# The last layer's bias for half the batch moves from matmuls into the factor

## The chip, the cores and the metric

The kernel runs on one core of one Trainium2 chip. The metric is the device time of one execution in microseconds (us), lower is better. A profile is one execution recorded by the hardware profiler; its span runs from the first to the last recorded instruction.

## The reference

A cross network of six layers over 4096 rows of 416 features, all in bf16:

```python
B, F, D, L = 4096, 26, 16, 6
Din = min(F * D, 1024)             # 416
x0: (B, Din)   ws: (L, Din, Din)   bs: (L, Din)

def reference(x0, ws, bs):
    x = x0
    for l in range(ws.shape[0]):
        x = x0 * (x @ ws[l] + bs[l]) + x
    return x
```

Every x is a product of x0 with a factor c: x = x0 * c, with c = 1 at the start and, after each layer, c = c + (x @ ws[l] + bs[l]). The kernel keeps c and forms x0 * c for the next layer's matmuls; the result is x0 times the last c.

## The kernel before

**Layout.** In layers 0 to 4 (L = 6, the last is `LL` = 5) features lie on partitions and batch rows in columns. The 416 features are three blocks of 128 (`m` or `k` = 0, 1, 2) and a remainder of 32. The batch is cut into two halves `s` = 0 and 1 of 2048 columns (`SW`), each of four groups `g` of 512 columns (`CW`). `CM[:, m, :]` holds the factor c for the blocks, `XM0` holds x0, and the `XH` buffers hold the products x0 * c that TensorE reads. The remainder lies in `CR` and `XR` with the four groups of a half on four groups of 32 partitions. `bM` and `bR` hold the biases of all layers in fp32, one value for each partition (one column for each layer), so the pair (`bM[:, m, l:l+1]`, or `bR[:, l:l+1]`) is a scalar for each partition.

**A layer from 1 to 4** has six tiles (s, m), in this order: (0,0), (0,1), (0,2), (1,0), (1,1), (1,2). The prediction calls them A, B, C, D, E, F, and the last of these layers (index 4, the fifth) layer five. They run in pairs: TensorE does the block matmuls of the first tile (`mm_full`, line 208), then the remainder's rows of the first and of the second (`mm_row`, line 214), then the block matmuls of the second. A tile's sums lie in two PSUM tiles (half `h` = 0 and 1, 1024 columns each). `ew_main` then does, for each half of a tile: ScalarE evicts PSUM into a buffer `t` and adds the bias (line 187); VectorE adds `t` to `CM` (line 188, the sum); VectorE multiplies `CM` by `XM0` into the next `XH` (line 189, the product). After the first pair, `rem_pair` does the remainder of both halves in the same way (`ew_rem`, lines 196, 202 and 203).

**What layer five adds.** The last layer is computed with batch rows on partitions, since the output has them so. So c is needed in rows too: after the eviction, sum and product of a tile's two halves, `xl_dmat` (line 231) issues one transposing DMA on SP's queue from `CM[:, m]` (2048 columns) into `XLrows`. For the remainder a transposing DMA goes from `CR` into `scrR[s]` (line 306), and ScalarE copies it into `XLrows` (`xl_rem`, line 313): for half 0 ahead of E's evictions, for half 1 after F's.

**The last layer.** Eight quads `q` = (s, i), four of each half; quad `q` covers four blocks of 128 batch rows (one in each group g), each with its own PSUM bank. They run two at a time (`rounds`: q = 0, 2, 4, 6), eight banks for each round. For each block TensorE multiplies the products (stationary) by the weights of the last layer (lines 361 and 367); `mm_q_rem` adds the remainder's features (line 379: four matmuls in four row groups) and the bias (line 382: four matmuls of a row of ones by the bias row `bLr`). ScalarE evicts into `t` (line 407), VectorE adds `XLrows` (line 409) and multiplies by x0 in rows into `o` (line 397), and a DMA on SP's queue writes `o` out. For the last three blocks of the last quad TensorE adds c itself (lines 371 and 373, by the identity), and the very last block is multiplied by VectorE straight from PSUM.

**What sets the order.** Each engine runs its instructions in one order. It follows the program's text; `pin` keeps the marked instructions in that order. SP's queue takes DMAs in the order in which they are issued. PSUM tiles come from one pool of four (two banks each), and `t` from a pool of six: a new tile waits until the one four, or six, before it has been read. The first eight banks of the last layer are those of E and F in layer five.

Of the kernel before, what the change touches and what calls it, by code (L numbers as in the profile page):

```python
# [9 lines left out]
ACT = mybir.ActivationFunctionType  # L10
ALU = mybir.AluOpType
BF16 = mybir.dt.bfloat16
FP32 = mybir.dt.float32
# [3 lines left out]
def kernel(  # L17
# [7 lines left out]
    nc = tc.nc  # L25
    B, D = x0.shape
    L = ws.shape[0]
    P = 128
    NK = 3
    R = D - NK * P  # L30
    assert R == 32 and B == 4096 and D == 416 and L >= 2
    NS = 2
    NG = 4
    CW = 512
    SW = NG * CW
    NBT = B // P
    LL = L - 1
# [3 lines left out]
    tpool = ctx.enter_context(tc.tile_pool(name="tpool", bufs=6))  # L41
    opool = ctx.enter_context(tc.tile_pool(name="opool", bufs=10))
    psum = ctx.enter_context(tc.tile_pool(name="psum", bufs=4, space=bass.MemoryType.PSUM))
# [8 lines left out]
    WR = const.tile([P, L, D], BF16)  # L52
# [3 lines left out]
    bM = const.tile([P, NK, L], FP32)  # L56
    bR = const.tile([P, L], FP32)
    X0rows = big.tile([P, NBT, D], BF16)
    XLrows = big.tile([P, NBT, D], BF16)
    scrR = [big.tile([P, 4, P], BF16, name=f"scrR{s}") for s in range(NS)]  # L60
# [3 lines left out]
    XM0 = big.tile([P, NK, B], BF16, name="XM0")  # L64
    XH = [big.tile([P, NK, SW], BF16, name=f"XH{i}") for i in range(3)]
    XR = [big.tile([P, NS * CW], BF16, name=f"XR{i}") for i in range(3)]
    CM = big.tile([P, NK, B], BF16, name="CM")
    CR = big.tile([P, NS * CW], BF16, name="CR")

    def col0(s, g):  # L70
        return SW * s + CW * g
# [8 lines left out]
    def pin(ins):  # L80
        tc.keep_in_program_order(ins)
# [94 lines left out]
    def ew_main(l, s, m, h, pt, nxt):  # L176
        c0 = col0(s, 2 * h)
        c, x = CM[:, m, c0:c0 + 2 * CW], nxt[s][:, m, 2 * CW * h:2 * CW * h + 2 * CW]
        src, bias = pt[:].rearrange("p a b -> p (a b)"), bM[:, m, l:l + 1]
        if l == 0:  # L180
            nc.scalar.activation(c, src, ACT.Identity, bias=bias, scale=1.0)  # L181
            for a in range(0, 2 * CW, CW):
                pin(nc.vector.tensor_tensor(out=x[:, a:a + CW], in0=c[:, a:a + CW],  # L183
                                            in1=XM0[:, m, c0 + a:c0 + a + CW], op=ALU.mult))
            return
        t = tpool.tile([P, 2 * CW], BF16, name="t")
        nc.scalar.activation(t[:], src, ACT.Identity, bias=bias, scale=1.0)  # L187
        nc.vector.tensor_tensor(out=c, in0=t[:], in1=c, op=ALU.add)  # L188
        nc.vector.tensor_tensor(out=x, in0=c, in1=XM0[:, m, c0:c0 + 2 * CW], op=ALU.mult)  # L189

    def ew_rem(l, s, pr, nxtR):
        cols = slice(CW * s, CW * s + CW)
        halves = [slice(a, a + CW // 2) for a in range(0, CW, CW // 2)]
        base = CR[:, cols] if l == 0 else tpool.tile([P, 2 * CW], BF16, name="t")
        for a in halves:
            nc.scalar.activation(base[:, a], pr[:, a], ACT.Identity, bias=bR[:, l:l + 1], scale=1.0)  # L196
        if l == 0:
            for a in halves:
                part = slice(CW * s + a.start, CW * s + a.stop)
                pin(nc.vector.tensor_tensor(out=nxtR[:, part], in0=CR[:, part], in1=XR[0][:, part], op=ALU.mult))  # L200
            return
        nc.vector.tensor_tensor(out=CR[:, cols], in0=base[:, 0:CW], in1=CR[:, cols], op=ALU.add)
        nc.vector.tensor_tensor(out=nxtR[:, cols], in0=CR[:, cols], in1=XR[0][:, cols], op=ALU.mult)

    def mm_full(l, s, m, g, pts, cur, first, last):
        for k in range(NK):
            for q in range(4):
                nc.tensor.matmul(pts[g // 2][32 * q:32 * q + 32, g % 2, :], lhsT=WM[:, l, k, 128 * m + 32 * q:128 * m + 32 * q + 32],  # L208
                                 rhs=cur[s][:, k, CW * g:CW * g + CW], start=(first and k == 0), stop=(last and k == NK - 1),
                                 tile_position=(0, 32 * q))  # L210

    def mm_row(l, s, m, pts, curR, first, last):
        for g in range(NG):
            nc.tensor.matmul(pts[g // 2][:, g % 2, :], lhsT=WR[32 * g:32 * g + 32, l, 128 * m:128 * m + 128],  # L214
                             rhs=curR[32 * g:32 * g + 32, CW * s:CW * s + CW],
                             start=first, stop=last, tile_position=(32 * g, 0))

    def mm_rem(l, s, pr, cur, curR):
        for g in range(NG):
            nc.tensor.matmul(pr[32 * g:32 * g + 32, :], lhsT=WD[:, l, g, :], rhs=curR[:, CW * s:CW * s + CW],  # L220
                             start=True, stop=False, tile_position=(0, 32 * g))
        for k in range(NK):
            for g in range(NG):
                nc.tensor.matmul(pr[32 * g:32 * g + 32, :], lhsT=WM[:, l, k, NK * P:D], rhs=cur[s][:, k, CW * g:CW * g + CW],  # L224
                      start=False, stop=(k == NK - 1), tile_position=(0, 32 * g))

    def new_pts():
        return [psum.tile([P, 2, CW], FP32, tag="ps", name=f"pt{h}") for h in range(2)]

    def xl_dmat(s, k):  # L230
        nc.sync.dma_start_transpose(out=XLrows[:, 16 * s:16 * s + 16, 128 * k:128 * k + 128],
                                    in_=CM[:, k, SW * s:SW * s + SW])
# [63 lines left out]
    for s in range(NS):  # L296
        first_layer(s)

    def rem_pair(l, cur, curR, nxtR, feeds_last):
        pr2 = psum.tile([P, 2, CW], FP32, tag="ps", name="pr2")  # L300
        for s in range(NS):
            mm_rem(l, s, pr2[:, s, :], cur, curR)
        for s in range(NS):
            ew_rem(l, s, pr2[:, s, :], nxtR)
            if feeds_last:
                nc.sync.dma_start_transpose(out=scrR[s][:], in_=CR[:, CW * s:CW * s + CW])

    def xl_rem(s):
        dst = XLrows[:, 16 * s:16 * s + 16, NK * P:D].rearrange("p (g i) r -> p i g r", g=NG)
        src = scrR[s][:].rearrange("p i (g r) -> p i g r", g=NG)  # L310
        n = 4 if s else 2
        for i in range(0, 4, n):
            pin(nc.scalar.copy(dst[:, i:i + n], src[:, i:i + n]))

    cur, curR = XH[0:2], XR[1]
    for l in range(1, LL):
        nxt, nxtR = [[h for h in XH if h is not cur[0] and h is not cur[1]][0], cur[0]], XR[1 + (l % 2)]
        feeds_last = (l == LL - 1)
        tiles = [(s, m) for s in range(NS) for m in range(NK)]
        pts = {}  # L320

        def finish(t):
            s, m = t
            for h in range(2):
                ew_main(l, s, m, h, pts[t][h], nxt)
            if feeds_last:
                xl_dmat(s, m)

        for n in range(0, len(tiles), 2):
            ta, tb = tiles[n], tiles[n + 1]  # L330
            pts[ta] = new_pts()
            for g in range(NG):
                mm_full(l, ta[0], ta[1], g, pts[ta], cur, True, False)
            mm_row(l, ta[0], ta[1], pts[ta], curR, False, True)
            pts[tb] = new_pts()
            mm_row(l, tb[0], tb[1], pts[tb], curR, True, False)
            if feeds_last and n == 4:
                xl_rem(0)
            finish(ta)
            for g in range(NG):  # L340
                mm_full(l, tb[0], tb[1], g, pts[tb], cur, False, True)
            finish(tb)
            if n == 0:
                rem_pair(l, cur, curR, nxtR, feeds_last)
        if feeds_last:
            xl_rem(1)
        cur, curR = nxt, nxtR

    l = LL
# [26 lines left out]
    def mm_q_rem(q, py, done):  # L376
        s, i = quads[q]
        for g in range(NG):
            nc.tensor.matmul(py[g][:, 0:D], lhsT=curR[32 * g:32 * g + 32, CW * s + 128 * i:CW * s + 128 * i + 128],  # L379
                             rhs=WR[32 * g:32 * g + 32, l, :], start=(g >= done), stop=False, tile_position=(32 * g, 0))  # L380
        for g in range(NG):
            nc.tensor.matmul(py[g][:, 0:D], lhsT=ones[32 * g:32 * g + 1, :],  # L382
                             rhs=bLr[32 * g:32 * g + 1, :], start=False, stop=(g < done), tile_position=(32 * g, 0))

# [32 lines left out]
    for q, at, done in rounds:  # L417
        tiles = [psum.tile([P, 2, CW], FP32, tag="ps", name=f"py{n}") for n in range(4)]
# [54 lines left out]
```

## Time and profile before

| | us |
|---|---|
| median of 3 runs | 130.15 (130.06 to 130.28) |
| profiled execution, device time | 129.88 |
| its span | 128.1 |
| TensorE busy | 123.6 |
| VectorE busy | 100.8 |
| ScalarE busy | 87.7 |

The granted TensorE clock is 1.0 throughout. The groups that the change touches, with count, busy time and mean duration of one, from the view of groups by form:

| line | engine, what | count | mean ns |
|---|---|---|---|
| 187 | ScalarE, eviction with bias, 128x1024 | 48 | 1114 |
| 188 | VectorE, sum, 128x1024 | 48 | 687 |
| 189 | VectorE, product, 128x1024 | 48 | 692 |
| 202, 203 | VectorE, remainder's sum and product, 128x512 | 8, 8 | 418, 425 |
| 379 | TensorE, remainder's features, last layer, 32x416 | 32 | 339 |
| 382 | TensorE, ones by bias, last layer, 1x416 | 32 | 335 |
| 407 | ScalarE, eviction, 128x832 and 128x416 | 9 and 13 | 855 and 505 |

A mean duration is not what an instruction costs its engine: the four matmuls of a group of line 379 or 382 run side by side, and one engine's instructions overlap at their ends, so the cost is read from the distance of starts.

### The profile page before, as it was taken

The numbers are of one execution on the slowest core, as the hardware profiler recorded it, in microseconds if no ns is written. First come the engines' busy times: TensorE is split into PE (matmuls) and PEld (weight loads), VectorE is DVE, ScalarE is ACT, GpSimd is POOL, SyncE is SP. The second block draws the span as 40 slices with busy tenths as digits, with TensorE's granted clock in tenths as the row PEclk, the third lists the DMA queues.
The fourth block names the chain that finished last, engine by engine and source line by source line (L and its number), as shares of the span: only waits on it lengthen the run. The fifth ranks groups of instructions, "written<-read, shape, count | busy, mean of one in ns | idle before, by whom it ended". The sixth has DMA issues, their size and how long they took to land.

```text
span 128.1 us, 4013 instructions
## 1 busy us (share of the span) xinstructions
PE 123.6 (97%) x1708; PEld 55.8 (44%) x1710; DVE 100.8 (79%) x195; ACT 87.7 (68%) x109; POOL 5.4 (4%) x18
## 2 busy tenths in 40 slices
PE   7999999999999999999999999999999999999980
PEld 3243443444544344434344434444434445445450
DVE  0034589774989898989898989898989899988991
ACT  0138857888858668858668858668858896569660
POOL 4004003400000000000000000000000000000000
PEclk9999999999999999999999999999999999999999
DMA  3999999999930000000000000000497899985764
GB/s 103 244 225 227 172 269 248 327 332 334 337 104 0 5 0 0 8 0 5 0 5 0 5 0 5 0 0 5 87 158 169 164 142 226 206 256 179 228 193 144
DMA packets 42230, 16.38 MB, mean 128 GB/s; under 512 B 31034, under 2 KB 42212, under 8 KB 42212
## 3 DMA queue, kind: packets, MB, share of 16 engines
q1 hardware_dynamic: 37432, 15.40, 53.2%
q10 hardware_dynamic: 4780, 0.72, 3.6%
q8 instruction: 13, 0.21, 0.7%
q14 instruction: 5, 0.04, 0.1%
HBM read 6.15 MB, written 3.41 MB: 75 GB/s over the span
## 4 chain that ended last, share of the span: by engine, by line
PE 96%; DVEq 1%; ACT 0%; issue 0%; DVE 0%
PE pt L208 50%; PE ph L240 12%; PE py L367 12%; PE pt L214 5%; PE pr L224 5%; PE wps L148 4%; PE pr L220 2%; PE py L379 1%; PE ph L247 1%; PE py L382 1%; PE py L361 1%; DVEq L468 1%; ACT t L407 0%; PE py L371 0%; PE tpr L163 0%
## 5 line engine op out<-in xcount | busy, mean ns | idle before, releaser
L208 PE MATMUL pt<-XH,WM 128*32 128x512 bf16 x1152 | 65.2, 379 | 0.0
L187 ACT ACTIVATE t<-pt,bM 128x1024 bf16<-128x1024 f32 x48 | 49.5, 1114 | 17.4 <-PE pt L214 17.4
L208 PEld LDWEIGHTS <-WM 128*32 128x32 bf16 x1152 | 29.7, 97 | 33.8 <-issue 5.1
L188 DVE TENSOR_TENSOR CM<-t,CM 128x1024 bf16<-128x1024 bf16 x48 | 33.0, 687 | 5.1 <-ACT t L187 5.1
L189 DVE TENSOR_TENSOR XH<-CM,XM 128x1024 bf16<-128x1024 bf16 x48 | 33.2, 692 | 3.6
L407 ACT CAST t<-py 128x416 bf16<-128x416 f32 (+1 forms) x22 | 14.3, 648 | 5.1 <-PE py L367 2.5
L367 PE MATMUL py<-WM,XH 128*128 128x416 bf16 x90 | 17.0, 339 | 0.0
L240 PE MATMUL ph<-XM,WM 128*128 128x512 bf16 x70 | 16.3, 380 | 0.1
L181 ACT ACTIVATE CM<-ph,bM 128x1024 bf16<-128x1024 f32 x12 | 12.5, 1113 | 3.5 <-PE ph L247 3.5
L183 DVE TENSOR_TENSOR XH<-CM,XM 128x512 bf16<-128x512 bf16 x24 | 8.8, 429 | 4.3 <-ACT CM L181 4.3
L367 PEld LDWEIGHTS <-XH 128*128 128x128 bf16 x90 | 8.5, 98 | 7.6 <-issue 1.4
L240 PEld LDWEIGHTS <-WM 128*128 128x128 bf16 x72 | 6.7, 98 | 8.4 <-issue 1.1
L409 DVE TENSOR_TENSOR t<-t,XLrows 128x416 bf16<-128x416 bf16 (+1 forms) x20 | 9.3, 468 | 1.1 <-ACT t L407 1.1
L397 DVE TENSOR_TENSOR o<-t,X0rows 128x416 bf16<-128x416 bf16 (+1 forms) x22 | 9.9, 457 | 0.1
L196 ACT ACTIVATE t<-pr,bR 128x256 bf16<-128x256 f32 x16 | 6.3, 474 | 2.1 <-PE pr L224 2.1
L214 PE MATMUL pt<-XR,WR 32*128 32x512 bf16 x96 | 7.3, 379 | 0.0
L224 PE MATMUL pr<-XH,WM 128*32 128x512 bf16 x96 | 6.6, 379 | 0.0
L114 ACT ACT_TABLE_LOAD x1 | 1.3, 1283 | 5.9 <-DMA XM<-in_x_dram 5.9
L224 PEld LDWEIGHTS <-WM 128*32 128x32 bf16 x120 | 3.2, 97 | 3.2
L157 DVE CAST bM<-pb 128x18 f32<-128x18 bf16 x1 | 0.2, 177 | 5.6 <-PE pb L156 5.6
L148 PE MATMUL wps<-const-float32-1.0 128*128 128x512 f32 x4 | 3.8, 1094 | 0.8 <-PEq L457 0.8
L220 PE MATMUL pr<-XR,WD 128*32 128x512 bf16 x40 | 3.9, 380 | 0.0
(53 smaller groups left out, 49.1 us busy)
## 6 DMA issues: line engine op xcount, KB each, us to landing
X0rows<-in_x_dram SPq DMA_DIRECT2D x8, 312.0 KB, 6.9
out_dram<-o SPq DMA_DIRECT2D x9, 208.0 KB, 3.3
WM<-in_ws_dram SPq DMA_DIRECT2D x5, 312.0 KB
out_dram<-o SPq DMA_DIRECT2D x13, 104.0 KB, 1.7
X0rows<-in_x_dram SPq DMA_DIRECT2D x4, 208.0 KB, 6.3
WR<-in_ws_dram SPq DMA_DIRECT2D x4, 130.0 KB, 5.3
WM<-in_ws_dram ACTq DMA_DIRECT2D x1, 312.0 KB
XM<-in_x_dram SPq DMA_TRANSPOSE x8, 5.5
```

The lines of the kernel that those rows point to most:

```text
L181: nc.scalar.activation(c, src, ACT.Identity, bias=bias, scale=1.0)
L187: nc.scalar.activation(t[:], src, ACT.Identity, bias=bias, scale=1.0)
L188: nc.vector.tensor_tensor(out=c, in0=t[:], in1=c, op=ALU.add)
L189: nc.vector.tensor_tensor(out=x, in0=c, in1=XM0[:, m, c0:c0 + 2 * CW], op=ALU.mult)
L208: nc.tensor.matmul(pts[g // 2][32 * q:32 * q + 32, g % 2, :], lhsT=WM[:, l, k, 128 * m + 32 * q:128 * m + 32 * q + 32], rhs=cur[s][:, k, C ...
L214: nc.tensor.matmul(pts[g // 2][:, g % 2, :], lhsT=WR[32 * g:32 * g + 32, l, 128 * m:128 * m + 128], rhs=curR[32 * g:32 * g + 32, CW * s:CW ...
L224: nc.tensor.matmul(pr[32 * g:32 * g + 32, :], lhsT=WM[:, l, k, NK * P:D], rhs=cur[s][:, k, CW * g:CW * g + CW], start=False, stop=(k == NK ...
L240: nc.tensor.matmul(pt[:, gl, :], lhsT=WM[:, 0, k, 128 * m:128 * m + 128], rhs=cur[:, k, c0:c0 + CW], start=(k == 0 and not after_row), sto ...
L367: nc.tensor.matmul(py[:, 0:D], lhsT=q_x(q, g, k), rhs=WM[:, l, k, :], start=((not closes) and k == 0), stop=(closes and not adds and k == ...
L397: pin(nc.vector.tensor_tensor(out=o[:, 0:n, :], in0=src, in1=X0rows[:, b, :], op=ALU.mult))
L407: nc.scalar.copy(tv, src)
L409: pin(nc.vector.tensor_tensor(out=tv, in0=tv, in1=XLrows[:, rows(q, g0, n), :], op=ALU.add))
```

## The change

In half 0 the last layer's bias is no longer added by TensorE. VectorE adds it to c in `CM` and `CR` in layer five, after the products that read c have been formed and before the transposing DMA takes c to rows: three tensor-with-scalar additions in place over 128x2048 (tiles A, B, C) and one over 128x512 (the remainder of half 0). In `mm_q_rem` the four matmuls by `ones` are left out for half 0 (the first four quads), and the remainder's matmuls close the accumulation there. Half 1 is as before.

Layer five gets a function of its own, `feeding_layer`, with VectorE's order written out and pinned. Sums stand ahead of products, other tiles' instructions stand between them, and the transposing DMAs of half 1 are issued after a tile's two sums, ahead of products. TensorE's order (`layer_products`) and ScalarE's order are those of before. On SP's queue the order is now A, remainder of half 0, B, remainder of half 1, C, D, E, F; before it was A, B, the two remainders, C, D, E, F. Layers 1 to 3 go through the same instructions as before.

```diff
+    def feeding_layer(l, cur, curR, nxt, nxtR):
...
+        def last_bias(c, bias):
+            pin(nc.vector.tensor_scalar(out=c, in0=c, scalar1=bias, scalar2=None, op0=ALU.add))
+
+        def rows_out(t):
+            s, m = t
+            if s == 0:
+                last_bias(CM[:, m, 0:SW], bM[:, m, LL:L])
+            xl_dmat(s, m)
+
+        A, Bt, C, Dt, E, F = tiles
+        layer_products(l, 0, tiles, pts, cur, curR, evict)
+        evict(Bt)
...
+        def rem_out(s):
+            part = slice(CW * s, CW * s + CW)
+            if s == 0:
+                last_bias(CR[:, part], bR[:, LL:L])
+            nc.sync.dma_start_transpose(out=scrR[s][:], in_=CR[:, part])
+
+        add(A, 0)
+        mul(A, 0)
+        add(A, 1)
+        add(Bt, 0)
+        mul(A, 1)
+        rows_out(A)
+        add(Bt, 1)
+        mul(Bt, 0)
+        rem(0, ALU.add)
+        mul(Bt, 1)
+        rem(0, ALU.mult)
+        rem_out(0)
+        rows_out(Bt)
+        rem(1, ALU.add)
+        rem_out(1)
+        rem(1, ALU.mult)
+
+        layer_products(l, 2, tiles, pts, cur, curR, evict)
+        evict(Dt)
+        add(C, 0)
+        add(C, 1)
+        mul(C, 0)
+        mul(C, 1)
+        rows_out(C)
+        add(Dt, 0)
+        add(Dt, 1)
+        rows_out(Dt)
+        mul(Dt, 0)
+        mul(Dt, 1)
+
+        def before_last(t):
+            xl_rem(0)
+            evict(t)
+
+        layer_products(l, 4, tiles, pts, cur, curR, before_last)
+        evict(F)
+        add(E, 0)
+        mul(E, 0)
+        add(E, 1)
+        rows_out(E)
+        add(F, 0)
+        mul(E, 1)
+        add(F, 1)
+        rows_out(F)
+        mul(F, 0)
+        mul(F, 1)
+        xl_rem(1)
...
         for g in range(NG):
             nc.tensor.matmul(py[g][:, 0:D], lhsT=curR[32 * g:32 * g + 32, CW * s + 128 * i:CW * s + 128 * i + 128],
-                             rhs=WR[32 * g:32 * g + 32, l, :], start=(g >= done), stop=False, tile_position=(32 * g, 0))
-        for g in range(NG):
+                             rhs=WR[32 * g:32 * g + 32, l, :], start=(g >= done), stop=(s == 0 and g < done),
+                             tile_position=(32 * g, 0))
+        for g in range(NG if s else 0):
             nc.tensor.matmul(py[g][:, 0:D], lhsT=ones[32 * g:32 * g + 1, :],
                              rhs=bLr[32 * g:32 * g + 1, :], start=False, stop=(g < done), tile_position=(32 * g, 0))
```

More of the change, by code (lines that the diff above doesn't have):

```diff
@@ L297, with rem_pair @@
         first_layer(s)
-    def rem_pair(l, cur, curR, nxtR, feeds_last):
+    def rem_pair(l, cur, curR, nxtR):
         pr2 = psum.tile([P, 2, CW], FP32, tag="ps", name="pr2")
@@ L304, in rem_pair @@
             ew_rem(l, s, pr2[:, s, :], nxtR)
-            if feeds_last:
-                nc.sync.dma_start_transpose(out=scrR[s][:], in_=CR[:, CW * s:CW * s + CW])
     def xl_rem(s):
@@ L313, in xl_rem, with layer_products @@
             pin(nc.scalar.copy(dst[:, i:i + n], src[:, i:i + n]))
+    def layer_products(l, n, tiles, pts, cur, curR, between):
+        ta, tb = tiles[n], tiles[n + 1]
+        pts[ta] = new_pts()
+        for g in range(NG):
+            mm_full(l, ta[0], ta[1], g, pts[ta], cur, True, False)
+        mm_row(l, ta[0], ta[1], pts[ta], curR, False, True)
+        pts[tb] = new_pts()
+        mm_row(l, tb[0], tb[1], pts[tb], curR, True, False)
+        between(ta)
+        for g in range(NG):
+            mm_full(l, tb[0], tb[1], g, pts[tb], cur, False, True)
@@ new lines, in feeding_layer, with evict, c_of, add @@
+    def feeding_layer(l, cur, curR, nxt, nxtR):
+        tiles = [(s, m) for s in range(NS) for m in range(NK)]
+        pts, ts = {}, {}
+        def evict(t):
+            for h in range(2):
+                ts[t + (h,)] = tpool.tile([P, 2 * CW], BF16, name="t")
+                nc.scalar.activation(ts[t + (h,)][:], pts[t][h][:].rearrange("p a b -> p (a b)"), ACT.Identity,
+                                     bias=bM[:, t[1], l:l + 1], scale=1.0)
+        def c_of(t, h):
+            c0 = col0(t[0], 2 * h)
+            return CM[:, t[1], c0:c0 + 2 * CW]
+        def add(t, h):
+            pin(nc.vector.tensor_tensor(out=c_of(t, h), in0=ts[t + (h,)][:], in1=c_of(t, h), op=ALU.add))
+        def mul(t, h):
+            c0 = col0(t[0], 2 * h)
+            pin(nc.vector.tensor_tensor(out=nxt[t[0]][:, t[1], 2 * CW * h:2 * CW * h + 2 * CW], in0=c_of(t, h),
+                                        in1=XM0[:, t[1], c0:c0 + 2 * CW], op=ALU.mult))
+        def last_bias(c, bias):
[8 more added lines that the diff above has]
+        evict(Bt)
+        pr2 = psum.tile([P, 2, CW], FP32, tag="ps", name="pr2")
+        for s in range(NS):
+            mm_rem(l, s, pr2[:, s, :], cur, curR)
+        tr = []
+        for s in range(NS):
+            tr.append(tpool.tile([P, 2 * CW], BF16, name="t"))
+            for a in range(0, CW, CW // 2):
+                nc.scalar.activation(tr[s][:, a:a + CW // 2], pr2[:, s, a:a + CW // 2], ACT.Identity, bias=bR[:, l:l + 1], scale=1.0)
+        def rem(s, op):
+            part = slice(CW * s, CW * s + CW)
+            if op == ALU.add:
+                pin(nc.vector.tensor_tensor(out=CR[:, part], in0=tr[s][:, 0:CW], in1=CR[:, part], op=op))
+            else:
+                pin(nc.vector.tensor_tensor(out=nxtR[:, part], in0=CR[:, part], in1=XR[0][:, part], op=op))
+        def rem_out(s):
+            part = slice(CW * s, CW * s + CW)
+            if s == 0:
[45 more added lines that the diff above has]
+        xl_rem(1)
@@ L317 @@
         nxt, nxtR = [[h for h in XH if h is not cur[0] and h is not cur[1]][0], cur[0]], XR[1 + (l % 2)]
-        feeds_last = (l == LL - 1)
+        if l == LL - 1:
+            feeding_layer(l, cur, curR, nxt, nxtR)
+            cur, curR = nxt, nxtR
+            break
         tiles = [(s, m) for s in range(NS) for m in range(NK)]
@@ L322, in finish @@
         def finish(t):
-            s, m = t
             for h in range(2):
-                ew_main(l, s, m, h, pts[t][h], nxt)
-            if feeds_last:
-                xl_dmat(s, m)
+                ew_main(l, t[0], t[1], h, pts[t][h], nxt)
         for n in range(0, len(tiles), 2):
-            ta, tb = tiles[n], tiles[n + 1]
-            pts[ta] = new_pts()
-            for g in range(NG):
[L333 to L342, printed above, removed]
+            layer_products(l, n, tiles, pts, cur, curR, finish)
+            finish(tiles[n + 1])
             if n == 0:
-                rem_pair(l, cur, curR, nxtR, feeds_last)
-        if feeds_last:
-            xl_rem(1)
+                rem_pair(l, cur, curR, nxtR)
         cur, curR = nxt, nxtR
@@ L379, in mm_q_rem @@
             nc.tensor.matmul(py[g][:, 0:D], lhsT=curR[32 * g:32 * g + 32, CW * s + 128 * i:CW * s + 128 * i + 128],
-                             rhs=WR[32 * g:32 * g + 32, l, :], start=(g >= done), stop=False, tile_position=(32 * g, 0))
-        for g in range(NG):
+                             rhs=WR[32 * g:32 * g + 32, l, :], start=(g >= done), stop=(s == 0 and g < done),
+                             tile_position=(32 * g, 0))
+        for g in range(NG if s else 0):
             nc.tensor.matmul(py[g][:, 0:D], lhsT=ones[32 * g:32 * g + 1, :],
```

## The prediction

> **What bounds the kernel now.** I read the first page first: which engine is busy, and who makes up the chain of work that ended last.
>
> ```profile
> span 128.1 us, 4013 instructions
> PE 123.6 (97%) x1708; PEld 55.8 (44%) x1710; DVE 100.8 (79%) x195; ACT 87.7 (68%) x109; POOL 5.4 (4%) x18
> ...
> PE 96%; DVEq 1%; ACT 0%; issue 0%; DVE 0%
> ```
>
> TensorE is the bound: busy for 123.6 of 128.1 us and 96% of the chain. So an edit counts if it shortens TensorE's own stream or makes TensorE wait. Next, the chain in order of time at the start of the last layer (start, length, what), for what the removed matmuls occupy:
>
> ```profile
> 104.42 0.29 PE py L379 x4
> 104.71 0.18 PE py L382 x4
> 104.88 0.18 PE py L379 x4
> 105.06 0.18 PE py L382 x4
> 105.24 4.33 PE py L367 x24
> ```
>
> Four L382 matmuls (the bias row, one per row group, side by side) take 0.18 us of the chain, once for each of the eight quads. Next, the timeline of the same place and of VectorE's way out of layer five (start, length, engine, line, idle time before):
>
> ```profile
> 103.48 1.12 ACT L187 ACTIVATE t<-pt,bM 128x1024 bf16<-128x1024 f32 x1
> ...
> 104.72 0.34 PE L379 MATMUL py<-WR,XR 32*128 32x416 bf16 x4
> ...
> 106.48 0.69 DVE L189 TENSOR_TENSOR XH<-CM,XM 128x1024 bf16<-128x1024 bf16 x1
> 107.09 1.09 DVE L409 TENSOR_TENSOR t<-t,XLrows 128x832 bf16<-128x832 bf16 x2
> ...
> 116.10 0.59 DVE L409 TENSOR_TENSOR t<-t,XLrows 128x832 bf16<-128x832 bf16 x1 [0.43 <-ACT t L407]
> ...
> 124.67 0.58 DVE L397 TENSOR_TENSOR o<-py,X0rows 128x416 bf16<-128x416 f32 x1
> ```
>
> Two things are to be seen. The last eviction of layer five ends at 103.48 + 1.12 = 104.60, and the second quad's first matmuls, which write the PSUM that it frees, start at 104.72: 0.12 us of slack. And VectorE goes from layer five to the last layer without idling (106.48, 107.09); it then waits for ScalarE three times, the last at 116.10, and from there to 124.67 its starts follow each other almost without a gap. So VectorE is a close second: work that is late there at 116.1 reaches the end.
>
> **The matmuls removed.** For batch half 0 the L382 matmuls go: 4 quads x 4 = 16 matmuls and 16 weight loads, in 4 groups of 0.18 us: 0.72 us. The 0.29 us at the entry to L379 and the 0.28 us from the last of them (104.89) to L367 (105.17) are at the change of matmul kind and stay. In the first pair of quads the second L379 would start at 104.54 rather than 104.72, but its PSUM is free at 104.60, and with some hundredths for the signal (VectorE starts 0.03 us after ScalarE in the chain's last steps) 0.1 us is lost again. I take 0.25 us for the first pair and 0.36 us for the second: **-0.6 us** on TensorE. In the second pair the eviction that frees the same PSUM (108.55 + 0.85 = 109.40) lies 0.47 us ahead of 109.87, so 0.18 us fits.
>
> **The bias on VectorE.** Four instructions come in: three over 128x2048 (tiles A, B, C, which are columns 0, 1 and 2 of half 0) and one over 128x512. The trace has no such operation. From 128x512 at 420 ns and 128x1024 at 687 ns, a two-input add costs 0.52 ns a column and 153 ns fixed. The nearest row is the one-source copy from SBUF to SBUF, L174, 64x512 in 288 ns: (288 - 153)/512 = 0.264 ns a column, so 0.69 us for 2048 columns and 0.29 us for 512. Upper bound: the row that reads fp32 from PSUM, 416 columns in 584 ns, 1.04 ns a column, gives 2.28 us; the two-input rate between gives 1.22 us and 0.42 us. None can be below nothing: they replace no VectorE work. I take 0.69 us, by the copy, which like these has one bf16 source in SBUF. An instruction that doesn't read what the one ahead has just written starts 0.08 us before that one's end (90.42 to 91.03, for 0.69), so the slots are 3 x 0.61 + 0.21 = 2.04 us.
>
> **The order on VectorE.** In the kernel before, each product follows its sum at once:
>
> ```profile
> 90.42 0.69 DVE L189 TENSOR_TENSOR XH<-CM,XM 128x1024 bf16<-128x1024 bf16 x1
> 91.03 0.69 DVE L188 TENSOR_TENSOR CM<-t,CM 128x1024 bf16<-128x1024 bf16 x1
> 91.75 0.69 DVE L189 TENSOR_TENSOR XH<-CM,XM 128x1024 bf16<-128x1024 bf16 x1
> 92.36 0.69 DVE L188 TENSOR_TENSOR CM<-t,CM 128x1024 bf16<-128x1024 bf16 x1
> 93.15 0.69 DVE L189 TENSOR_TENSOR XH<-CM,XM 128x1024 bf16<-128x1024 bf16 x1
> ```
>
> A product behind its own sum starts 0.72 or 0.79 us after it, a sum behind another tile's product 0.61 us. In the new order ten of twelve products have something between, which saves 10 x 0.145 = 1.45 us, and so has one of two remainder products (0.45 against 0.34). The waits for ScalarE ahead of C's and E's sums (0.36 and 0.23 us, and at each the 0.08 us of overlap) are filled as well. Laid out one by one from 88.23, with each eviction's end as the earliest start of its sum: A's bias starts at 91.46, the remainder's at 94.58, B's at 94.80, C's first sum at 96.20, C's bias at 98.64, E's first sum at 101.69 (its eviction ends at 101.59), the last product at 106.11. VectorE is free at 106.7 instead of 107.09. So the four biases cost **nothing**, hidden by the removed dependency gaps (1.56 us) and waits (0.75 us), 2.31 us against 2.04. Without that cover they would move 107.09 to 109.1. ScalarE's order doesn't change, and each of the six t buffers it writes has been read by a sum well before (C's evictions, from 94.64, need A's sums).
>
> The Trainium skill speaks against this part: the page "VectorE: DVE Perf Modes", section "The DRAIN you can't avoid", has the next operation held until the pipe is empty, whatever the semaphores. By that, order would buy nothing; the trace has starts 0.08 us ahead of the previous end where there is no dependency, so here I go by the trace, and keep the rule as a rival.
>
> **The transposes.** Each moves on SP's queue. A's is issued at 92.15 (after its bias) instead of 90.34, and the remainder's first goes ahead of B's:
>
> ```profile
> 94.92 3.65 SPq L306 DMA_TRANSPOSE scrR<-CR  x2
> 98.67 11.49 SPq L231 DMA_TRANSPOSE XLrows<-CM  x4
> ```
>
> ScalarE's copies from scrR stand ahead of E's evictions, and those end 0.12 us before TensorE needs them; but scrR's first issue comes at 94.87, as before (94.92), now with only A's transfer ahead of it, so it lands no later than its 99.13. Behind it, with the issue times of before (2.34, 1.75, 1.22, 1.87, 3.72, 2.57 us), C is issued at about 100.2 and F at 108.3 instead of 98.67 and 107.10; with 4.5 us to landing they are there at 104.7 and 112.8. Their readers are the adds at 106.7 and at 115.5: 2 us of slack each. The outputs queued behind F start some 1.1 us later (110.25 to 111.4); ten o buffers are first reused at about 117.3, when the first output has long landed (3.3 us). So: nothing. TensorE's inputs are safe too: half 0's last product is done by 98.8 (first read 103.2), half 1's by 106.8 (first read 114).
>
> **Sum.** Profiled execution 129.88 us (span 128.1, 1.8 around it): 129.88 - 0.6 = 129.28. The median of the runs, 130.15, lies 0.27 above the profiled one: 130.15 - 0.6 = **129.55 us**, span 127.5.
>
> **Rivals.** (1) VectorE takes the end: slower. If the bias runs at the two-input rate, it costs 3 x 0.53 + 0.13 = 1.72 us more, and VectorE is free at 108.4. Sixteen instructions of 0.50 us follow before the add that was at 116.10, so it starts at 116.5, 0.4 later than before and 1 us later than TensorE would allow (115.5). From there VectorE has under 0.2 us of idling in all: 130.35 to 130.55, say 130.4; at the upper bound, 2.28 us, 3 x 1.06 us later still, 133.6. It decides as soon as VectorE leaves layer five more than 0.7 us behind my 106.7 (115.5 - 8.05 = 107.4), and turns into a loss from 108.1. For: no tensor-with-scalar row of that size in the trace. Against: L174. The skill's rule works the same way: starts no closer than about 0.70 us in the new order give 109.2 at the end of layer five and 131.1; the starts of 0.61 speak against it. (2) The gain is hidden: the transposes land 2 us later than I have them (D's issue alone took 3.72 us, so the queue does back up), the adds at 106.7 or 115.5 wait, and VectorE's lateness takes back what TensorE gained: 130.1. Against: the transfers leave gaps of their own (DMA share 0.11 from 96 to 97 us). (3) More is gained: the second L379 isn't held by the eviction, 0.72 us, 129.4; inside the forecast's own range.
>
> **How the numbers follow.** Forecast with (3): 0.72, its own range 129.3 to 129.8. (2): 0.14, 129.9 to 130.4. (1) with the rule: 0.14, 130.4 and above. About 0.2% (0.26 us) is what a measurement can tell from no change, so faster 0.72, same 0.15, slower 0.13. The range reaches through (2) to the edge of (1): 129.3 to 130.4.
>
> **What would show it.** L382 with 16 matmuls; the first L367 of the last layer about 0.25 us earlier than 105.17, the next entry to L379 after q=2 0.6 us earlier; the four biases at 0.69 and 0.29 us; VectorE's first L409 at or before 107.1 with no wait on a DMA; the last direct product near 124.05. I am wrong if the bias takes 1.2 us, if adds wait for XLrows, if TensorE idles at the entry to the last layer, or if the last L397 doesn't move although L367 does.

## The result and the profile after

The changed kernel takes 129.49 us (median of 8 runs, 129.19 to 129.78) against 130.0 us (129.75 to 130.3, 8 runs) for the kernel before, run beside it: ratio 0.9956, 95% interval 0.9938 to 0.9973. The prediction was 129.55 us, range 129.3 to 130.4, with a chance of 0.72 for faster by over 0.2%. So the gain is 0.51 us where 0.6 was forecast. That the time itself came closer, to 0.06 us, is chance: the kernel before took 130.0 us in these runs, and the forecast had started from 130.15.

The page of the profile after, to be laid beside the first lines of before:

```profile
span 127.8 us, 3986 instructions
PE 123.0 (96%) x1692; PEld 55.5 (43%) x1694; DVE 102.3 (80%) x199; ACT 87.6 (69%) x109; POOL 5.0 (4%) x18
```

Sixteen matmuls and sixteen weight loads fewer, four VectorE instructions more. The chain in order of time at the first two pairs of quads (start, length, what; the matmuls of line 379 are now line 480, those of line 367 line 468):

```profile
104.47 0.59 PE py L480 x8
105.06 4.33 PE py L468 x24
109.39 0.46 PE py L480 x8
109.85 4.33 PE py L468 x24
```

From the entry to the next L468 it takes 0.59 and 0.46 us where before it took 0.82 (104.42 to 105.24 in the lines shown there). TensorE gains 0.23 and 0.36 us. VectorE's timeline (start, length, engine, line, idle time before; L340 is the sum, L344 the product, L348 the bias, L511 and L499 the last layer's add and multiplication):

```profile
90.90 0.69 DVE L344 TENSOR_TENSOR XH<-CM,XM 128x1024 bf16<-128x1024 bf16 x1
91.62 0.75 DVE L348 TENSOR_SCALAR CM<-CM,bM 128x2048 bf16<-128x2048 bf16 x1
92.29 0.68 DVE L340 TENSOR_TENSOR CM<-t,CM 128x1024 bf16<-128x1024 bf16 x1
92.89 0.69 DVE L344 TENSOR_TENSOR XH<-CM,XM 128x1024 bf16<-128x1024 bf16 x1
...
107.15 1.08 DVE L511 TENSOR_TENSOR t<-t,XLrows 128x832 bf16<-128x832 bf16 x2
...
115.59 0.59 DVE L511 TENSOR_TENSOR t<-t,XLrows 128x832 bf16<-128x832 bf16 x1 [0.45 <-ACT t L509]
...
124.13 0.59 DVE L499 TENSOR_TENSOR o<-py,X0rows 128x416 bf16<-128x416 f32 x1
```

Three things are to be seen. A bias takes 0.75 us and a slot of 0.67 (91.62 to 92.29). VectorE leaves layer five at 107.15, practically when it did before (107.09), with four instructions more behind it. And the last product starts at 124.13 instead of 124.67: 0.54 us of the 0.59 that TensorE gained, since layer five began 0.05 us later in this execution.

The spans differ by less than that, 128.1 against 127.8 us. Before, 3.43 us follow the start of the last product, and here 3.67. The end follows SP's last output: it is issued at 125.14 before and at 124.84 here, and in both the span ends 3.0 us behind it. In the second trace of the changed kernel (the run that took it again, below) the last product starts at 124.12, SP's last output is issued at 124.59, and the span is 127.5 us.

### The profile page after: what moved, and what is told of

Read it like the earlier page. It is cut to its first block, busy times and chain, and to the rows that moved or that the text cites. A ratio compares the mean times of both kernels' runs of the same rounds, so it can differ in the third digit from the quotient of the medians.

```text
span 127.8 us, 3986 instructions
## 1 busy us (share of the span) xinstructions
PE 123.0 (96%) x1692; PEld 55.5 (43%) x1694; DVE 102.3 (80%) x199; ACT 87.6 (69%) x109; POOL 5.0 (4%) x18
## 4 chain that ended last, share of the span: by engine, by line
PE 90%; DMA 4%; ACTq 2%; DVEq 1%; issue 0%; ACT 0%; DVE 0%
PE pt L208 50%; PE py L468 12%; PE ph L240 11%; PE pt L214 5%; PE pr L224 5%; DMA xrig<-in_x_dram 4%; PE pr L220 2%; PE py L480 2%; PE ph L247 1%; PE py L462 1%; ACTq L86 1%; PE py L484 1%; DVEq L570 1%; ACTq L108 1%; ACT t L509 0%
## 5 line engine op out<-in xcount | busy, mean ns | idle before, releaser
L468 PE MATMUL py<-WM,XH 128*128 128x416 bf16 x90 | 17.0, 339 | 0.0
L468 PEld LDWEIGHTS <-XH 128*128 128x128 bf16 x90 | 8.5, 98 | 7.5 <-issue 1.2
L499 DVE TENSOR_TENSOR o<-t,X0rows 128x416 bf16<-128x416 bf16 (+1 forms) x22 | 9.9, 458 | 0.1
L511 DVE TENSOR_TENSOR t<-t,XLrows 128x416 bf16<-128x416 bf16 (+1 forms) x20 | 9.3, 468 | 0.6 <-ACT t L509 0.6
L340 DVE TENSOR_TENSOR CM<-t,CM 128x1024 bf16<-128x1024 bf16 x12 | 7.9, 685 | 0.3 <-ACT t L332 0.3
L344 DVE TENSOR_TENSOR XH<-CM,XM 128x1024 bf16<-128x1024 bf16 x12 | 8.0, 686 | 0.1
L196 ACT ACTIVATE t<-pr,bR 128x256 bf16<-128x256 f32 x12 | 4.7, 474 | 1.6 <-PE pr L224 1.6
```

Of the source, the lines that this page charges most:

```text
L468: nc.tensor.matmul(py[:, 0:D], lhsT=q_x(q, g, k), rhs=WM[:, l, k, :], start=((not closes) and k == 0), stop=(closes and not adds and k == ...
L499: pin(nc.vector.tensor_tensor(out=o[:, 0:n, :], in0=src, in1=X0rows[:, b, :], op=ALU.mult))
```

## The experiments

Each ran beside the kernel before on the same chip, and ratios are to that one.

**The matmuls alone.**

```diff
-                             rhs=WR[...], start=(g >= done), stop=False, tile_position=(32 * g, 0))
-        for g in range(NG):
+                             rhs=WR[...], start=(g >= done), stop=(s == 0 and g < done), tile_position=(32 * g, 0))
+        for g in range(NG if s else 0):
```

> The kernel before with the 16 matmuls by ones of batch half 0 left out and nothing added: the last layer's bias for half 0 is left out of the computation. Theory (TensorE's removed matmuls are the whole gain, VectorE only has to keep out of the way): VectorE leaves layer five at 107.1 as before, which is early enough, and the time is 129.4 to 129.5 against 130.0 before, like the changed kernel; the last product on VectorE starts near 124.1. Rival (the new order on VectorE is what gains): no change, 130.0.

129.37 us, ratio 0.9963 (0.9952 to 0.9974); first add of the last layer at 107.15, last product at 124.15. That is the changed kernel's gain without any of its VectorE work. Within the intervals, the removed matmuls are the whole gain.

**The order alone.** The changed kernel without the biases, with all matmuls:

```diff
-            if s == 0:
-                last_bias(CM[:, m, 0:SW], bM[:, m, LL:L])
...
-            if s == 0:
-                last_bias(CR[:, part], bR[:, LL:L])
...
-                             rhs=WR[...], start=(g >= done), stop=(s == 0 and g < done),
+                             rhs=WR[...], start=(g >= done), stop=False,
...
-        for g in range(NG if s else 0):
+        for g in range(NG):
```

> The change's order on VectorE and SP without the bias additions, and with all matmuls by ones: TensorE's work is that of before. Theory (order alone only makes VectorE earlier): first add of the last layer at about 106.6 instead of 107.09, time 129.9 to 130.1, no change. Rival (order itself gains): 129.5 or less.

129.99 us, ratio 1.0009 (0.9999 to 1.0018); first add at 106.77, last product at 124.78. No change, as the theory had it: the order gains nothing by itself.

**The biases in the old order.** The kernel before with the biases ahead of its transposing DMAs and without the sixteen matmuls:

```diff
             if feeds_last:
+                if s == 0:
+                    last_bias(CM[:, m, 0:SW], bM[:, m, LL:L])
                 xl_dmat(s, m)
...
             if feeds_last:
+                if s == 0:
+                    last_bias(CR[:, 0:CW], bR[:, LL:L])
                 nc.sync.dma_start_transpose(out=scrR[s][:], in_=CR[:, CW * s:CW * s + CW])
```

> The four bias additions and the left-out matmuls of the change, but VectorE keeps the order of before (each product right behind its sum). Theory (VectorE has no room beyond about 107.4 at the end of layer five, and only the new order makes room for the biases): the four slots (2.3 us) and the waits behind the products (0.4) less the idle time that they fill (0.75) put VectorE's first add of the last layer at about 109.0; the add that was at 116.10 starts at about 117, and the kernel is slower than before, 130.5 to 130.9. Rival (VectorE isn't near being the bound, the order is of no account): 129.4 to 129.5.

130.36 us, ratio 1.0034 (1.0022 to 1.0046): slower, a little less than expected, and not only for the expected reason. VectorE's first add is at 108.77 and the add of round q=4 at 116.33, not 117. But something else happened, in the timelines of ScalarE and of TensorE (the last bracket is the idle time before, and who ended it):

```profile
100.66 0.71 ACT L318 COPY XLrows<-scrR 128x256 bf16<-128x256 bf16 x2 [1.95 <-DMA scrR<-CR]
101.28 4.12 ACT L187 ACTIVATE t<-pt,bM 128x1024 bf16<-128x1024 f32 x4
```

```profile
104.29 0.52 PE L386 MATMUL py<-WR,XR 32*128 32x416 bf16 x6
105.45 0.35 PE L386 MATMUL py<-WR,XR 32*128 32x416 bf16 x2 [0.63 <-ACT t L187]
```

ScalarE waits 1.95 us for the remainder's transposing DMA, E's and F's evictions start 0.8 us late behind it, and TensorE stands idle for the PSUM: its next block matmuls start at 105.73, where in the changed kernel they start at 104.99. So two causes were mixed, VectorE's lateness and the late remainder. The next runs separate them.

**Only VectorE late.** The changed kernel, its queue order kept, each product behind its own sum again:

```diff
         add(A, 0)
         mul(A, 0)
         add(A, 1)
-        add(Bt, 0)
         mul(A, 1)
         rows_out(A)
+        add(Bt, 0)
+        mul(Bt, 0)
         add(Bt, 1)
-        mul(Bt, 0)
+        mul(Bt, 1)
...
```

> The changed kernel with SP's new order kept, but on VectorE each product right behind its sum again. Theory (VectorE is a close second: late at the end of layer five by more than about 0.5 us, it reaches the end): first add of the last layer at about 108.8, no wait on scrR and no idle TensorE at the entry, the add of round q=4 at about 116.3 instead of 115.6, last product at about 124.7, time 129.9 to 130.1, the gain used up. Rival (what cost the run with the old order its time was only the late scrR): 129.4 to 129.5.

130.35 us, ratio 1.003 (1.0019 to 1.0042): the gain is not only used up, the kernel is slower than before. ScalarE waits for no DMA and TensorE isn't idle at the entry. VectorE's timeline:

```profile
109.03 1.09 DVE L511 TENSOR_TENSOR t<-t,XLrows 128x832 bf16<-128x832 bf16 x2
...
116.56 0.58 DVE L511 TENSOR_TENSOR t<-t,XLrows 128x832 bf16<-128x832 bf16 x1
...
124.92 0.58 DVE L499 TENSOR_TENSOR o<-py,X0rows 128x416 bf16<-128x416 f32 x1
```

No line from 109.03 on has a wait: VectorE runs without a break, and the last product comes 15.89 us after the first add.

**Only the remainder late.** First the remainder's DMA was written behind B's, with nothing to fix the order (`rem_out` keeps the bias alone here, and `rem_dma` issues the DMA):

```diff
-        rem_out(0)
-        rows_out(Bt)
-        rem(1, ALU.add)
-        rem_out(1)
+        rem_out(0)
+        rows_out(Bt)
+        rem_dma(0)
+        rem(1, ALU.add)
+        rem_dma(1)
```

> The changed kernel with one thing put back: on SP's queue the remainder's transposing DMA of half 0 stands behind B's again. VectorE's order is that of the change. Theory (ScalarE's copies from scrR stand ahead of E's evictions, so a late landing of scrR holds the evictions, and these the last layer's first PSUM): the DMA is issued at about 97.8 instead of 95.3 and lands at about 101 to 102; E's first eviction starts 0.6 to 1.8 us later than 100.5, TensorE idles 0.5 to 1.7 us at the entry to the last layer, and the time is 129.9 to 131.1. Rival (the place in the queue is of no account, the order on VectorE is what matters): 129.4 to 129.5, like the changed kernel.

129.42 us, ratio 0.996 (0.9948 to 0.9973), and this says nothing on the question: SP still issued A, the remainder, B (92.51, 95.41, 97.23), though the text has B first. So an instruction that isn't pinned need not stay where the text has it; that it is placed when its data are ready would explain this, but isn't shown. The run is one more of the changed kernel. With the DMAs pinned as well:

```diff
-            xl_dmat(s, m)
+            pin(xl_dmat(s, m))
...
-            nc.sync.dma_start_transpose(out=scrR[s][:], in_=CR[:, CW * s:CW * s + CW])
+            pin(nc.sync.dma_start_transpose(out=scrR[s][:], in_=CR[:, CW * s:CW * s + CW]))
```

> As the run before it with the old queue order, but with the DMAs pinned, so that the remainder's transposing DMA of half 0 really stands behind B's; VectorE's order is that of the change. Theory (a late scrR holds ScalarE, ScalarE holds PSUM, PSUM holds TensorE): the DMA is issued at about 98 and lands at 100.6 to 101.1, ScalarE waits some 2 us for it, E's first eviction starts at 101.2 to 101.7 instead of 100.5, TensorE idles 0.5 to 1 us at the entry to the last layer, last product at 124.7 to 125.1 instead of 124.1, time 130.0 to 130.4. Rival (place in the queue of no account): 129.4 to 129.5.

130.62 us, ratio 1.0052 (1.0038 to 1.0065), more than expected. B's DMA is issued at 95.87 for 2.93 us, the remainder's at 98.90. ScalarE and TensorE:

```profile
101.41 0.71 ACT L311 COPY XLrows<-scrR 128x256 bf16<-128x256 bf16 x2 [2.64 <-DMA scrR<-CR]
102.03 4.12 ACT L332 ACTIVATE t<-pt,bM 128x1024 bf16<-128x1024 f32 x4
```

```profile
105.19 0.35 PE L483 MATMUL py<-WR,XR 32*128 32x416 bf16 x2 [0.48 <-ACT t L332]
106.20 0.35 PE L483 MATMUL py<-WR,XR 32*128 32x416 bf16 x2 [0.65 <-ACT t L332]
106.48 4.39 PE L471 MATMUL py<-WM,XH 128*128 128x416 bf16 x24
```

ScalarE waits 2.64 us. TensorE stands idle for 0.48 + 0.65 = 1.13 us, and its matmuls no longer overlap there, so the next block matmuls start at 106.48 and not at 104.99: 1.49 us are lost, two and a half times what the removed matmuls give, and the last product is as much later (125.62 against 124.13). VectorE does the same work in the same order as in the change and still waits for ScalarE three times behind layer five, so it isn't what sets the end. So the place of one small DMA in SP's queue is worth more than all sixteen matmuls. What pinning does by itself was not run; that it isn't the cause is argued from the run in the old order, where no DMA was pinned and ScalarE waited 1.95 us in the same place.

**Both halves on VectorE.** All eight biases, no matmul by ones, the DMAs of half 1 behind their bias:

```diff
-            if s == 0:
-                last_bias(CM[:, m, 0:SW], bM[:, m, LL:L])
+            last_bias(CM[:, m, SW * s:SW * s + SW], bM[:, m, LL:L])
...
-        for g in range(NG if s else 0):
-            nc.tensor.matmul(py[g][:, 0:D], lhsT=ones[...], ...)
```

> The change carried on to half 1: eight bias additions on VectorE, no matmul by ones at all, the transposing DMAs of half 1 behind their bias. Theory (VectorE becomes the bound): 0.72 us less on TensorE, but VectorE leaves layer five at about 109.8, 2.4 us behind what the last layer has room for, and the end moves with it: 131.2 to 131.7. Rival (TensorE stays the bound whatever VectorE does): 128.8 to 128.9.

131.2 us, ratio 1.0097 (1.0082 to 1.0111). VectorE's timeline:

```profile
110.10 1.08 DVE L506 TENSOR_TENSOR t<-t,XLrows 128x832 bf16<-128x832 bf16 x2
...
125.99 0.58 DVE L494 TENSOR_TENSOR o<-py,X0rows 128x416 bf16<-128x416 f32 x1
```

Again 15.89 us from the first add to the last product without a wait, with four more groups of 0.18 us taken from TensorE: VectorE is the bound here.

**Half 1 on GpSimd.** As the run before, with half 1's four biases on the engine that is idle then:

```diff
+            eng = nc.gpsimd if s else nc.vector
-            pin(nc.vector.tensor_scalar(out=c, in0=c, scalar1=bias, scalar2=None, op0=ALU.add))
+            pin(eng.tensor_scalar(out=c, in0=c, scalar1=bias, scalar2=None, op0=ALU.add))
```

> The change carried on to half 1, whose four bias additions are on GpSimd, which is idle then; no matmul by ones at all. GpSimd's nearest row is a copy of 416 columns in 529 ns, so 2048 columns take some 2 to 2.6 us. Theory A (GpSimd works beside VectorE unhindered): VectorE as in the changed kernel, TensorE 0.72 us less, F's rows land at about 114.5, in time: 128.7 to 128.9. Theory B (the two engines keep each other out of SBUF, as the Trainium skill, page "SBUF — State Buffer", has it for their shared port pair): VectorE loses 2 to 8 us in layer five and the kernel ends at 131 to 136.

141.74 us, ratio 1.091 (1.0893 to 1.0927): worse than either theory. From GpSimd's and VectorE's timelines:

```profile
102.77 5.81 POOL L349 TENSOR_SCALAR CM<-CM,bM 128x2048 bf16<-128x2048 bf16 x1 [3.55 <-DVE XH L344]
```

```profile
103.31 4.08 DVE L344 TENSOR_TENSOR XH<-CM,XM 128x1024 bf16<-128x1024 bf16 x1
```

One bias over 128x2048 takes GpSimd 6.07 us on average. Beside each of the three, one VectorE instruction takes 4.01 to 4.12 us instead of 0.58 or 0.69, some 3.4 us more; that is 10.2 us in all, and the run is 11.8 us slower than the kernel before. Behind the second and the third, ScalarE waits up to 4.17 us for VectorE's products, and TensorE up to 3.94 us for ScalarE. The Trainium skill has it (page "SBUF — State Buffer", section "SBUF: two separate sides") that the port pair which the two engines share is an exclusive lock, held for a whole instruction. The trace agrees in part: VectorE is held, but only in one instruction for each of GpSimd's, while the others beside it take their usual time, and the lock itself isn't seen.

**As far as VectorE has room.** The change, and of half 1 the biases of tile D and of the remainder, with matmuls by ones over the other 256 columns; biases moved so that none stands right behind a product of the same tile:

```diff
-            if s == 0:
+            if s == 0 or m == 0:
-                last_bias(CM[:, m, 0:SW], bM[:, m, LL:L])
+                last_bias(CM[:, m, SW * s:SW * s + SW], bM[:, m, LL:L])
...
+            nc.tensor.matmul(py[g][:, P:KD], lhsT=ones[...], rhs=bLr[32 * g:32 * g + 1, P:KD], ...)
```

> The change carried on as far as VectorE has room. In half 1 VectorE also adds the bias of tile D (feature block 0) and of the remainder; the matmuls by ones of half 1 cover feature blocks 1 and 2 only, 256 columns instead of 416. Two more slots on VectorE (0.67 + 0.27 us); no bias stands right behind a product of the same tile any more (three waits of 0.11 us less). Theory (the last product is at the later of TensorE's schedule and 15.9 us after VectorE leaves layer five, as the runs with both halves and with adjacent pairs had it): VectorE leaves at 107.6 to 107.9, with room to 108.0; TensorE gains 4 x 0.18 x 160/416 = 0.28 us more; last product at about 123.85, time 129.1 to 129.3, 0.2 to 0.3 us below the changed kernel. Rival (VectorE has no room left, as the prediction had it: at most 107.4): 129.5 to 129.9. Rival (a short matmul doesn't take less): 129.4 to 129.5.

> The changed kernel once more, beside the two others of this set: 129.4 to 129.5 by every theory.

129.32 us, ratio 0.9951 (0.9935 to 0.9967), beside 129.33, 0.9954 (0.9942 to 0.9966), for the change itself in the same set: the 0.2 to 0.3 us that were expected are not seen in the time. Inside the kernel most of it is there: VectorE leaves layer five at 107.52, with two more biases, and a pair of quads takes 0.69 us from the entry to the next L467 (114.17 to 114.86) where the change takes 0.82. The last product starts at 123.93 against 124.12. It can't start earlier, since VectorE has no wait left behind this line:

```profile
115.56 0.59 DVE L520 TENSOR_TENSOR t<-t,XLrows 128x832 bf16<-128x832 bf16 x1 [0.36 <-ACT t L518]
```

From the same add to the last product the run with adjacent pairs, in which VectorE never waits, takes 124.92 - 116.56 = 8.36 us, and 115.56 + 8.36 = 123.92. And the end didn't follow the last product: SP issues its last outputs back to back, the last at 124.55 against 124.59, and both spans are 127.5 us. In eleven of the twelve traces so far the span ends 2.9 to 3.0 us after SP's last issue; the exception is the run on GpSimd, with 3.4. So two runs moved one of the last outputs to ScalarE's queue:

```diff
-            ew(..., nc.scalar if final and u == 7 else nc.sync, ...)
+            ew(..., nc.scalar if final and u in (5, 7) else nc.sync, ...)
```

> The kernel of the run with part of half 1 on VectorE, and the output of the third block from the end goes out on ScalarE's queue instead of SP's, so that SP has three of the last five outputs and ScalarE two. Theory (in that run the last product came 0.2 us earlier but SP issued the last outputs back to back, 0.47 us apart, and the end follows SP's last issue by 2.95 us): SP's last issue at about 124.1 to 124.3 instead of 124.55, the end then follows ScalarE's issue at 124.54 by 2.8 us, span 127.3, time 129.0 to 129.2. Rival (the time that TensorE gained was never there): 129.3 to 129.4.

> The changed kernel with that output on ScalarE's queue alone. Theory: ScalarE's last issue (124.75) already lands as late as SP's (124.6 to 124.84), so little or nothing: 129.2 to 129.45. Rival (SP's issue of the outputs sets the end of the changed kernel as well): 129.0 to 129.2.

129.54 us, 0.9968 (0.9952 to 0.9983), and 129.72 us, 0.9979 (0.9967 to 0.9991): both theories fall, it is no gain. SP's last issue comes at 124.12 and 124.33, 0.3 to 0.5 us earlier than in the runs without the move, and yet the spans are 127.7 and 127.9 us: the end now follows SP's last issue by 3.6 us, and ScalarE's (124.60 and 124.72) by 3.1 and 3.2. What sets it then is left open. Whether the move is a loss can't be told either, since the two kernels without it ran in another set. No run was faster than the change by more than its interval.

## Why the prediction was right, point by point

**The matmuls removed: right.** 0.6 us was forecast, 0.25 of it in the first pair and 0.36 in the second; the chain shows 0.23 and 0.36. The 0.13 us by which the first pair is worse than the second is the forecast hold by the last eviction, which ends at 103.54 + 1.12 = 104.66 here. The last two matmuls of the entry, which write PSUM that it frees, start at 104.71, 0.05 us later. In the two runs with the late remainder, where the trace names ScalarE as what these matmuls wait for, they also start 0.05 us behind that eviction's end (105.40 to 105.45, and 106.15 to 106.20). The run with the matmuls alone shows that nothing else gains.

**The bias on VectorE: right in kind, short in size.** Groups of the changed kernel (count, busy us, mean ns):

```profile
L348 DVE TENSOR_SCALAR CM<-CM,bM 128x2048 bf16<-128x2048 bf16 x3 | 2.3, 752 | 0.1
L348 DVE TENSOR_SCALAR CR<-CR,bR 128x512 bf16<-128x512 bf16 x1 | 0.4, 353 | 0.0
```

(752 - 353)/1536 = 0.26 ns a column, the copy's rate; the fixed part is 0.22 us instead of 0.153. The term was 3 x 0.61 + 0.21 = 2.04 us and measured 3 x 0.67 + 0.27 = 2.28.

**The order on VectorE: right, with one gap left over.** Sums behind sums and products behind products start 0.60 us apart, so the rule that the pipe must empty first, which the prediction weighed and set aside, doesn't hold for these. The prediction had read that section of the Trainium skill (page "VectorE: DVE Perf Modes", section "The DRAIN you can't avoid") by half: it goes on to say that a next operation which isn't held back starts earlier. The 0.60 us agree with that, so the section taken whole was no rival. But a bias right behind a product that only reads the same c starts 0.72 us after it (90.90 to 91.62), and the remainder's 0.45 (94.43 to 94.88). The forecast counted a gap only where an instruction reads what the one ahead has written; writing in place over what the one ahead reads has it too. In the run with part of half 1, where another tile's sum stands ahead of the same bias, the gap is gone:

```profile
91.56 0.69 DVE L340 TENSOR_TENSOR CM<-t,CM 128x1024 bf16<-128x1024 bf16 x1
92.16 0.75 DVE L348 TENSOR_SCALAR CM<-CM,bM 128x2048 bf16<-128x2048 bf16 x1
```

Three such gaps of 0.11 to 0.12 us and the longer slots (0.24 us) are why VectorE left at 107.15 and not at 106.7; of these 0.6 us, starts that are 0.60 and not 0.61 us apart give some back. The order was needed: without it (the run with adjacent pairs) VectorE leaves at 109.03, and the kernel is slower than before. That the forecast's sentence on lost cover has 109.1 is chance: it lost the filled waits (0.75 us) as well, which that run keeps, and had shorter slots and none of these gaps.

**VectorE's room: the step that was mis-sized.** The prediction let VectorE leave layer five at 107.4 at the latest for the full gain, with a loss from 108.1. Two runs in which VectorE never waits give 15.89 us from the first add to the last product; the changed kernel's last product is at 124.13, so the room ends at 124.13 - 15.89 = 108.24, and a loss begins at 124.67 - 15.89 = 108.78. The forecast counted sixteen instructions between the first add and that of round q=4, and there are fifteen (109.03 to 116.56 is 7.53 us, not 8.05); most of the rest is what VectorE still waits behind that add, 8.54 us in the changed kernel against 8.36. So there were two errors of opposite sign: VectorE came out of layer five 0.45 us later than forecast, and it had 0.8 us more room. The forecast margin of 0.7 us would have covered the first alone; the real one was 108.24 - 107.15 = 1.09 us. The rival's price is off by the same step: it put the end at 130.4 us for VectorE leaving at 108.4, where the measured rule gives a last product at 108.4 + 15.89 = 124.29, still ahead of before; 130.35 us came only at 109.03. In the run with the biases in the old order, which leaves at 108.77, the rule gives 124.66, as early as before. Its last product comes at 124.87, and that is TensorE's doing: the block matmuls of round q=4 start 0.20 us later than before (115.67 against 115.47), and the last product is 0.20 us later. There it was the late remainder, and not VectorE, that made the loss.

**The transposes: right, and more was at stake than was said.** C and F were issued at 101.14 and 109.97, later than the forecast 100.2 and 108.3, and no add waited for `XLrows`. The remainder's DMA came at 95.30 (forecast 94.87), and ScalarE copied from scrR without waiting (in the second trace of the change it waited 0.19 us, and E's evictions started as early, at 100.52):

```profile
98.72 0.71 ACT L311 COPY XLrows<-scrR 128x256 bf16<-128x256 bf16 x2
```

The prediction named ScalarE's copies from scrR ahead of E's evictions, and rightly found that the remainder's new place in the queue keeps them in time. But its rival of late transposes looked for the wait at VectorE's adds alone, and put no price on the place in the queue. The runs with the old order and with the pinned queue show the price: a late remainder holds ScalarE, and from there TensorE. The place ahead of B is what makes biases ahead of the DMAs affordable.

## What to carry to other kernels

When work goes from the busiest engine to the second, find out how late the second may be: let it run without waits from that point and subtract the time from the end that the first engine allows (here 124.13 - 15.89). What makes room on an engine with short dependent instructions is independent work between them, 0.11 to 0.18 us for each pair. And look at what stands behind a small transfer on the engine that waits for it: an eviction queued behind a copy that waits for a DMA carries that DMA's lateness into PSUM, and so to TensorE. A gain at the last instruction of an engine isn't yet one at the end: here the end followed the last output that SP issued, and a kernel whose last product came 0.19 us earlier took as long.

## What the hardware showed that was not expected

- GpSimd needs 6.07 us for a tensor-with-scalar addition over 128x2048 bf16 that takes VectorE 0.75 us, and 2.35 us for one over 128x512, though its copy of 32x416 takes 0.53 us. One VectorE instruction beside each of the long ones takes 4.01 to 4.12 us.
- A VectorE addition over 128x2048 in place starts 0.72 us after a product over 128x1024 that only reads the same c, and 0.60 us after a sum of another tile.
- In the run on GpSimd the granted TensorE clock, 1.0 until then, was 0.61 from 116 to 120 us, 0.50 from 120 to 124 and 0.61 from 124 to 128. TensorE had been busy for 2.43 of the 4 us from 112 on and for 0.50 of the 4 us from 116 on.
- Issuing one of SP's transposing DMAs takes 1.2 to 3.7 us; on what it depends isn't shown. Put behind B's, the remainder's small one was issued 3.6 us later (98.90 against 95.30), and ScalarE's copy from it started at 101.41 instead of 98.7 to 99.0.
- The span ends 2.9 to 3.0 us after SP's last output is issued, in eleven traces. With one of the last outputs moved to ScalarE's queue it was 3.6 us; why is open.
